# Where a seed is copied and where a shared product is added: a seven-product scheme between ScalarE and VectorE

## The chip, the cores and the metric

The kernel runs on one core of a Trainium2 chip. The core has five engines that work through queues of their own and wait for each other by semaphores: TensorE (PE, matmuls), VectorE (DVE), ScalarE (ACT), GpSimd (POOL) and SyncE (SP, which issues most DMAs). The metric is the time of one execution in microseconds; the median of three runs is compared.

## The reference

```python
def _A_ref(x, wqkv, wo):                  # x: 2048 x 640
    H = 32; Dh = D // H                   # 32 heads of 20
    W, dil = 8, 2
    qkv = ((x @ wqkv).reshape(B, S, 3, H, Dh)).transpose(2, 0, 3, 1, 4)
    q, k, v = qkv[0], qkv[1], qkv[2]
    idx = pos[:, None] - off[None, :]     # each position sees 8 keys, 2 apart, itself the last
    ...
    logits = einsum("bhsd,bhswd->bhsw", q, kg) * Dh ** -0.5
    attn = softmax(where(mask, logits, -1e9))
    o = einsum("bhsw,bhswd->bhsd", attn, vg)
    return o.transpose(0, 2, 1, 3).reshape(B, S, D) @ wo

def _B_ref(x, w1, b1, w2):                # Dense 640 -> 1728, Mish, Dense 1728 -> 640
    h = einsum("bsd,df->bsf", x, w1) + b1
    act = h * tanh(softplus(h))
    return einsum("bsf,fd->bsd", act, w2)

g = sigmoid((x * gate_w).sum(-1, keepdims=True))
return g * _A_ref(x, wqkv, wo) + (1 - g) * _B_ref(B_x, ...)
```

In this kernel both branches read the same `x`.

## The kernel before

**Matmuls.** Each float32 operand is split into a high and a low part that lie together in a `pair` buffer; a product takes three matmuls (high x high, high x low, low x high, in `mm3`, L519 to L521). ScalarE makes the high part (L451), VectorE or GpSimd the low part (L454). Matrix products are formed where possible by a seven-product scheme on 2 x 2 blocks, in which sums of blocks are multiplied and the products are added up in PSUM.

**Units.** The projection to q, k and v is worked in eight units `u`, four groups of eight heads for each half `P` of the positions, and each unit in eight slots of 128 positions. Units 2 and 3, and 6 and 7, are worked together by class `Two` (tokens `p.2.…` and `p.6.…`), in which part of the products follow the seven-product scheme, for four column blocks `j`. For each `j` there are seven steps: `a1` forms the shared product `ep` and has it copied to SBUF (`v`, an `hb` buffer), `a2` starts the sum `al`, and `be` begins with `al` plus the shared product; `a3` adds a product to `be`, `b1` and `b2` finish `al` and `be`. `c0` to `c3` do the same for the second unit from stored partial sums (`pu`, `pv`): `ga` begins with a copy (L887), `de` begins with `ga` minus the stored `v`. The value with which a PSUM bank begins is its seed here. Seeds of `Two` are made by VectorE in one instruction that reads a bank and an SBUF buffer and writes the other bank (`sum_to`, L833), 16 times in all: two for each of four `j` in both pairs of units.

When a slot's sum is done, `qkv_evac` reads it out by three ScalarE copies: k and v (320 columns, L687), q (160 columns, L689) and 16 columns of the first dense layer (`hx`, L691); a fourth (L693) only in the first unit of each half.

**Other quads.** The first dense layer is worked in quads (tokens `q.…`, classes `Quad`, `Single`, `Plain`). Their seeds already are ScalarE copies from bank to bank (`Quad.seed`, L1142), and the shared product is added by VectorE when a block is read out (`Quad.added`, L1160).

**Attention** (`attention`) runs on VectorE for each half of a unit: products with the keys (L576), sums over the 20 elements of a head (L579), maximum (L597), subtraction (L598), the exponential on ScalarE (L599), weights times the gate on ScalarE into `pw` in SBUF (L603, four instructions), sum, reciprocal and the product of both into `pg` in PSUM (L610 to L612), products with the values (L621) and their sums (L625). `qg` is a PSUM copy of two slots of q (L582); `pg` and `qg` take one bank each, and the other six are the buffers `qb` and `sb`, three each.

**Order.** `ORDER` is a list of tokens that sets the order of TensorE's work. The other engines' orders are worked out by `Plan.run`, which goes through the tasks with their ranks, estimated times and due times, and gives tasks marked "ANY" to VectorE or GpSimd (`PATIENCE` is the time after which VectorE takes one that nothing of TensorE waits for). `BANKS` names the ring (`qb` or `sb`) for some of the banks, and `NPAIR` is the number of pair buffers. After planning each engine's instructions run strictly in the planned order. Waits between engines are set by the tiles that instructions touch.

Of the kernel before, what the change touches and what calls it, by code (L numbers as in the profile page):

```python
# [17 lines left out]
KC = D // 128  # L18
# [48 lines left out]
class Plan:  # L67


    NEAR, PATIENCE = 6000, 1000  # L70
# [178 lines left out]
NPAIR, NRAW, NH = 24, 8, 6  # L249
# [4 lines left out]
BANKS = {'q1500': 's', 'p20ga': 'q', 'u04': 's', 'p21de': 's', 'u45': 's', 'p61ga': 'q', 'p63be': 'q', 'p63de': 's', 'q04ep': 's', 'q1210': 'q', 'p60de': 's', 'q1010': 'q', 'q1200': 's', 'q1111': 's', 'q02al': 's', 'u07': 's', 'u06': 's', 'q1410': 'q', 'q1501': 'q', 'u41': 's', 'q1411': 's', 'l3': 's', 'l0': 's', 'q1401': 'q', 'u46': 's', 'q1311': 's', 'q1201': 'q', 'u05': 's', 'u43': 's', 'q1001': 'q', 'u44': 's', 'q1101': 'q'}  # L254
C_RINGS = 'sqsqsqqq'
ORDER = """
u.0.6 u.0.5 last.0 u.0.4 u.0.7 q.0.0.first pieces.0.1 q.0.0.m1 q.0.1.first q.0.1.second q.0.0.second q.0.0.m3 q.0.0.m4 q.0.1.m1 wq.1 last.1 q.0.0.l2
q.0.0.m2 q.0.0.l1 pieces.0.2 q.0.1.m2 q.0.1.m4 q.0.1.m3 u.1.0 q.0.2.first u.1.2 u.1.3 u.1.1 q.0.1.l1 u.1.7 sum u.1.6 u.1.4 u.1.5 q.0.2.m1 q.0.1.l2
q.0.2.second q.0.2.m3 wa.2 q.0.2.m4 pieces.0.3 p.2.0.a1 p.2.1.a1 sum q.0.2.l2 q.0.2.m2 p.2.0.a2 p.2.0.a3 p.2.0.b1 p.2.1.a2 p.2.1.b1 p.2.1.a3 q.0.2.l1
p.2.2.a1 p.2.2.a2 p.2.2.a3 p.2.3.a1 p.2.0.b2 p.2.2.b2 p.2.3.a2 p.2.1.b2 p.2.3.b1 p.2.3.a3 q.0.3.first pieces.0.4 q.0.3.m1 q.0.3.second p.2.2.b1 wc.2  # L260
q.0.3.m3 q.0.3.m4 q.0.3.m2 p.2.3.b2 q.0.4.second q.0.3.l1 p.2.1.c0 q.0.4.first q.0.3.l2 q.0.4.m1 p.2.0.c0 q.0.4.m4 q.0.4.m3 q.0.4.m2 pieces.0.5
p.2.3.c0 x.2.0 q.0.4.l1 q.0.5.first x.2.2 q.0.5.m1 x.3.3 p.2.2.c0 x.2.1 x.3.1 q.0.4.l2 q.0.5.m4 x.3.4 x.2.3 q.0.5.m2 q.0.5.second p.2.3.c1 q.0.5.m3
p.2.3.c2 x.2.4 p.2.2.c1 q.0.5.l2 p.2.0.c1 wq.4 p.2.3.c3 x.3.2 x.3.0 q.0.5.l1 p.2.1.c1 p.2.1.c2 p.2.2.c3 p.2.2.c2 p.2.0.c3 p.2.0.c2 pieces.1.0 p.2.1.c3
third u.4.0 u.4.5 u.4.7 q.1.0.m2 sum u.4.1 wq.5 u.4.3 q.1.0.second u.4.2 sum q.1.0.m1 rest.0 u.4.6 sum rest.1 pieces.1.1 u.4.4 sum pieces.1.2 u.5.1
q.1.0.first q.1.1.first u.5.5 u.5.0 sum q.1.1.second lastw.1 q.1.1.m2 u.5.7 pieces.1.4 u.5.6 sum u.5.2 pieces.1.3 q.1.2.second q.1.1.m1 q.1.2.first
sum q.1.2.m2 u.5.4 q.1.2.m1 q.1.4.first q.1.3.first q.1.3.second pieces.1.5 last.2 u.5.3 q.1.3.m2 q.1.3.m1 q.1.4.second q.1.4.m2 forms.1.0 q.1.4.m1
last.3 wa.6 q.1.5.second p.6.1.a1 p.6.0.a1 q.1.5.m1 q.1.5.m2 p.6.0.a2 p.6.0.a3 wc.6 p.6.1.a2 p.6.0.b2 q.1.5.first p.6.2.a1 p.6.2.a2 p.6.3.a1 p.6.2.a3
p.6.0.c0 p.6.1.a3 p.6.0.b1 p.6.3.a2 p.6.0.c1 p.6.1.b1 p.6.2.b1 p.6.3.b1 p.6.2.b2 p.6.1.c0 p.6.1.c1 p.6.0.c3 p.6.3.a3 p.6.3.b2 p.6.2.c0 p.6.1.c3
p.6.3.c0 p.6.0.c2 p.6.2.c1 p.6.3.c1 p.6.2.c3 p.6.2.c2 p.6.1.c2 p.6.3.c3 p.6.1.b2 p.6.3.c2 rest.2 rest.3
# [4 lines left out]
def kernel(ctx: ExitStack, tc: tile.TileContext, x, wq, wo, w1, b1, w2, out):  # L274
# [109 lines left out]
    bound = keep.tile([1, HQ, 7], F32)  # L384
    zt = keep.tile([128, 2, 8], F32)
    gate = keep.tile([128, 2, 8], F32)
    gc = keep.tile([128, 2, 32], F32)
    gt = keep.tile([128, 2, 32], F32)
# [1569 lines left out]
```

## Time and profile before

| | |
|---|---|
| median of 3 runs | 623.35 us (620.57 to 626.04) |
| the profiled execution | 619.11 us, its span 617.3 us |
| TensorE busy | 610.7 us (99%) |
| VectorE busy | 584.2 us (95%), 551 instructions |
| ScalarE busy | 375.6 us (61%), 875 instructions |
| GpSimd busy | 335.8 us (54%) |
| DMA | 151.83 MB, 246 GB/s |

A row of a group gives the line, the engine, the operation, output and inputs by the program's names, the shape and the count, then the busy time in us and the mean ns of one, and last the idle time of the engine just before these instructions and what ended it. A row of the timeline gives start and duration in us, and in brackets the idle time ahead and what ended it. A row of the waits gives who waited for whom, us in total, times, and the longest. A row of stretches (from:to, length) gives the busy time of PE, PEld (weight loads), DVE, ACT and POOL with their counts, the granted clock of TensorE, the DMA share and GB/s.

### The profile page before, as it was taken

Reading aid. Unit: us, or ns where it says so; the run is one execution under the profiler, and the core shown is the slowest. Engines: PE = TensorE matmul, PEld = TensorE weight load, DVE = VectorE, ACT = ScalarE, POOL = GpSimd, SP = SyncE. Lnnn points to the kernel's source line nnn. Section 1 sums busy time; section 2 is a strip of 40 time slices with the busy share of each in tenths; the row PEclk is TensorE's granted clock in tenths of the full one; section 3 lists DMA queues with packets and bytes.
Section 4 is the critical chain, followed back from the end, with each engine's and each line's share of the span. In section 5 each row is a group of like instructions: output and inputs, shape, how many; then the busy total and the mean of one; then the engine's idle time right before and its main releaser. Section 6 shows DMA issues by size and latency. Waiting matters only on the chain.

```text
span 617.3 us, 9163 instructions
## 1 busy us (share of the span) xinstructions
PE 610.7 (99%) x2707; PEld 506.3 (82%) x2707; DVE 584.2 (95%) x551; ACT 375.6 (61%) x875; POOL 335.8 (54%) x309
## 2 busy tenths in 40 slices
PE   9999999999999999999999999999999999999997
PEld 7887888888878888888888888888888888888886
DVE  8799999999999999999999999999999999989955
ACT  6677747766797574654557559567686534664520
POOL 1587847868887546666887508886516824001000
PEclk9999999999999999999999999999999999999999
DMA  9773784979989679999999889868787876899613
GB/s 322 222 217 104 218 289 124 272 245 299 327 252 287 209 234 248 290 272 342 300 256 299 273 264 311 251 181 256 222 273 249 218 230 181 254 288 352 237 52 119
DMA packets 99971, 151.83 MB, mean 246 GB/s; under 512 B 11265, under 2 KB 52481, under 8 KB 99697
## 3 DMA queue, kind: packets, MB, share of 16 engines
q1 hardware_dynamic: 96560, 145.48, 73.4%
q0 software_dynamic: 3072, 5.51, 6.2%
q8 instruction: 21, 0.34, 0.2%
q10 hardware_dynamic: 288, 0.26, 0.2%
q14 instruction: 30, 0.24, 0.1%
HBM read 95.17 MB, written 55.06 MB: 243 GB/s over the span
## 4 chain that ended last, share of the span: by engine, by line
PE 91%; DVE 5%; ACT 2%; issue 1%; DMA 0%; SPq 0%; DVEq 0%; ACTq 0%
PE qb L521 16%; PE qb L520 16%; PE qb L519 16%; PE sb L519 14%; PE sb L521 13%; PE sb L520 13%; DVE pr L576 2%; DVE lg L579 1%; DVE raw L1025 1%; ACT pair L451 1%; PE qb L681 1%; PE sb L433 1%; DMA raw<-in_wq 0%; DVE pair L454 0%; PE sb L525 0%
## 5 line engine op out<-in xcount | busy, mean ns | idle before, releaser
L454 POOL TENSOR_TENSOR pair<-raw,pair 128x512 fp32r<-128x512 f32 (+3 forms) x143 | 176.1, 1254 | 99.4 <-ACT pair L451 64.1
L451 ACT ACTIVATE pair<-raw 128x512 fp32r<-128x512 f32 (+3 forms) x236 | 137.3, 606 | 56.1 <-DMA raw<-actt 12.7
L519 PE MATMUL sb<-pair 128*128 128x512 f32 (+2 forms) x386 | 149.7, 388 | 0.9 <-ACT sb L1142 0.4
L519 PE MATMUL qb<-pair 128*128 128x512 f32 (+1 forms) x387 | 150.0, 388 | 0.5 <-DVE qb L833 0.5
L521 PE MATMUL qb<-pair 128*128 128x512 f32 (+1 forms) x387 | 149.9, 387 | 0.0
L520 PE MATMUL qb<-pair 128*128 128x512 f32 (+1 forms) x387 | 149.8, 387 | 0.0
L521 PE MATMUL sb<-pair 128*128 128x512 f32 (+2 forms) x386 | 149.2, 387 | 0.0
L520 PE MATMUL sb<-pair 128*128 128x512 f32 (+2 forms) x386 | 149.2, 387 | 0.0
L621 DVE TENSOR_TENSOR pr<-kvq,pg 128x1280 f32<-128x1280 f32 x64 | 93.2, 1483 | 0.9
L576 DVE TENSOR_TENSOR pr<-kvq,qg 128x2560 f32<-128x2560 f32 x32 | 89.9, 2811 | 1.4
L625 DVE TENSOR_REDUCE kvq<-pr 128x320 f32<-128x2560 f32 x32 | 90.1, 2817 | 0.8
L579 DVE TENSOR_REDUCE lg<-pr 128x128 f32<-128x2560 f32 x32 | 90.2, 2818 | 0.8
L519 PEld LDWEIGHTS sb<-pair 128*128 128x128 f32 x386 | 72.5, 188 | 17.1 <-DVE sb L833 1.0
L519 PEld LDWEIGHTS qb<-pair 128*128 128x128 f32 x387 | 72.6, 188 | 15.4 <-DVE qb L833 0.9
L520 PEld LDWEIGHTS qb<-pair 128*128 128x128 f32 x387 | 72.7, 188 | 14.4
L521 PEld LDWEIGHTS qb<-pair 128*128 128x128 f32 x387 | 72.7, 188 | 14.3
L521 PEld LDWEIGHTS sb<-pair 128*128 128x128 f32 x386 | 72.5, 188 | 14.5
L520 PEld LDWEIGHTS sb<-pair 128*128 128x128 f32 x386 | 72.5, 188 | 14.4
L454 DVE TENSOR_TENSOR pair<-raw,pair 128x512 fp32r<-128x512 f32 (+3 forms) x93 | 65.7, 730 | 3.0 <-ACT pair L451 2.9
L1025 POOL TENSOR_TENSOR hb<-hb 128x512 f32<-128x512 f32 x34 | 44.6, 1327 | 12.2 <-DVE pg L612 3.1
L1025 POOL TENSOR_TENSOR raw<-raw 128x256 f32<-128x256 f32 (+2 forms) x35 | 34.9, 1002 | 12.2 <-DVE pg L612 3.0
L451 ACT ACTIVATE pair<-hb 128x512 fp32r<-128x512 f32 (+3 forms) x62 | 36.5, 589 | 1.7 <-PE qb L521 1.5
(167 smaller groups left out, 739.0 us busy)
## 6 DMA issues: line engine op xcount, KB each, us to landing
actt<-hb SPq DMA_DIRECT2D x52, 256.0 KB
raw<-in_w SPq DMA_DIRECT2D x47, 256.0 KB
act<-hb SPq DMA_DIRECT2D x38, 256.0 KB
raw<-in_wq SPq DMA_DIRECT2D x39, 248.0 KB
raw<-actt SPq DMA_DIRECT2D x37, 256.0 KB
raw<-act SPq DMA_DIRECT2D x29, 256.0 KB
raw<-in_x SPq DMA_DIRECT2D x27, 256.0 KB
o<-ot SPq DMA_DIRECT2D x64, 80.0 KB
```

What stands on the lines that cost most here:

```text
L433: nc.tensor.matmul(warm_banks[i % 3].t[:, :n], ones[:, :128], ones[:, :n], start=True, stop=True)
L451: a = add("ACT", act_ns(n), lambda: A.activation(hi(), raw(), AF.Copy), after, rank=rank, take=take, hold=hold)
L454: return (V if e == "DVE" else G).tensor_tensor(lo(), raw(), hi().bitcast(F32), op=OP.subtract)
L519: nc.tensor.matmul(ps, ah, bh, start=first, stop=False, skip_group_check=more)
L520: nc.tensor.matmul(ps, ah, bl, start=False, stop=False, skip_group_check=more)
L521: nc.tensor.matmul(ps, al, bh, start=False, stop=last, skip_group_check=more)
L576: return V.tensor_tensor(pr, window(kv, s0, 0), qg[:, :, None, :].to_broadcast([128, 2, W, QF]), op=OP.mult)
L579: V.tensor_reduce(lg_w[:, s0:s0 + 2], pr.rearrange("p s w (h d) -> p s w h d", d=DH), op=OP.add, axis=AX.X)
L621: V.tensor_tensor(pairs[:, s].rearrange("p k i (h d) -> p k i h d", d=DH), vw, pg[:, s0 + s].rearrange("p (k i) h -> p k i h", i=2)[:, :, ...
L625: V.tensor_reduce(q[:, s0:s0 + 2], pairs.rearrange("p s k i f -> p s f k i"), op=OP.add, axis=AX.XY)
L681: nc.tensor.matmul(ps.t[:, :n], X[0, kc].t[:, a, i * 128:(i + 1) * 128], WQ[0, kc].t[:, b, :n], start=a == b and kc == 0, stop=False)
L1025: return (V if e == "DVE" else G).tensor_tensor(t.t[:, i:i + n], a.t[:, j:j + n], b.t[:, k:k + n], op=op)
```

## The change

The seed in `Two` becomes a ScalarE copy from bank to bank (`seed`, in place of `sum_to`), in `a2` and in `c1`. The shared product is no longer part of the seed: VectorE adds or, through the stored `v`, takes it in when the slot is read out (`qkv_evac_added`), for `b2` and `c2`, 16 read-outs in all, with three additions each in place of three ScalarE copies. The sum `de` in `c3` is read out by ScalarE as before, since its seed needs `v` only through `ga`. `a2` no longer waits for `a1`.

In `attention` the weights times the gate are written into `pg` in PSUM at once, and their product with the reciprocal is made there in place; `pw` is gone. The maxima `mx` move from SBUF into the PSUM tile of `qg`. `bound`, `gc` and `gt` are smaller. With the room that this leaves there are 25 pair buffers in place of 24. `PATIENCE` goes from 1000 to 2000, and `ORDER` and `BANKS` are new lists.

```diff
-    NEAR, PATIENCE = 6000, 1000
+    NEAR, PATIENCE = 6000, 2000
...
-NPAIR, NRAW, NH = 24, 8, 6
+NPAIR, NRAW, NH = 25, 8, 6
...
-    pw = at.tile([128, 8, W, HQ], F32, name="pw")
-    pw_h = pw.rearrange("p s w h -> p s h w")
     pg = shared.tile([128, 8, W, HQ], F32, name="pg")
-    qg = shared.tile([128, 2, QF], F32, name="qg")
+    pg_h = pg.rearrange("p s w h -> p s h w")
+    qm = shared.tile([128, 512], F32, name="qg")
+    qg = qm[:, :2 * QF].rearrange("p (s f) -> p s f", f=QF)
...
-    mx = at.tile([128, 8, HQ], F32, name="mx")
+    mx = qm[:, 2 * QF:2 * QF + 8 * HQ].rearrange("p (s h) -> p s h", h=HQ)
...
-                    A.activation(pw_h[:, i], lg[:, i], AF.Copy, scale=gate[:, P, i:i + 1])
+                    A.activation(pg_h[:, i], lg[:, i], AF.Copy, scale=gate[:, P, i:i + 1])
...
-            return t, step("DVE", 430, lambda: V.tensor_tensor(pg[:, h], pw[:, h], sm[:, h, None, :].to_broadcast([128, 4, W, HQ]), op=OP.mult), [copied])
+            return t, step("DVE", 430, lambda: V.tensor_tensor(pg[:, h], pg[:, h], sm[:, h, None, :].to_broadcast([128, 4, W, HQ]), op=OP.mult), [copied])
...
+    def qkv_evac_added(u, P, hq, i, ps, done, more, held, landed):
+        kv, q, s = KV[UNIT[u]], Q[UNIT[u]], 4 * (1 - i // 4) + i % 4
...
+        def plus(to, lo, n, after):
+            return add("DVE", dve_ns(n), lambda: V.tensor_tensor(to(), ps.t[:, lo:lo + n], more()[:, lo:lo + n], op=OP.add), after,
+                       rank=SOON, kind="psum", hold=[ps, held])
+
+        def pair():
+            return V.tensor_tensor(kv[:, 7 + s], ps.t[:, QF:3 * QF].rearrange("p (a b) -> p a b", a=2),
+                                   more()[:, QF:3 * QF].rearrange("p (a b) -> p a b", a=2), op=OP.add)
+
+        a = add("DVE", dve_ns(2 * QF), pair, [done, landed] + before, rank=SOON, kind="psum", hold=[ps, held])
+        b = plus(lambda: q[:, s], 0, QF, [a])
+        c = plus(lambda: hx[:, P, i, hq], 3 * QF, RQ, [b])
...
-        def sum_to(self, to, x, y, op, n, after, yt=None):
-            yt = yt or (lambda: y.t)
-            return add("DVE", dve_ns(n) + 80, lambda: V.tensor_tensor(to.t[:, :n], x.t[:, :n], yt()[:, :n], op=op), after, rank=SOON, kind="psum",
-                       take=[to], hold=[to, x, y])
+        def seed(self, to, of, n, after):
+            return add("ACT", act_ns(n) + 60, lambda: A.activation(to.t[:, :n], of.t[:, :n], AF.Copy), after, rank=-0.5, take=[to], hold=[to, of])
...
-            self.seeded[j] = self.sum_to(be, al, self.v[j], OP.add, n, [t, self.copied[j]])
+            self.seeded[j] = self.seed(be, al, n, [t])
...
         def b2(self, j):
             t = self.products(self.be[j], j, self.xs("s4", 1, 1) + self.plain(0, 1), [self.kept[j]], self.n)
-            units[self.u].ready(4 + j, self.be[j], t)
+            v = self.v[j]
+            units[self.u].ready(4 + j, self.be[j], t, lambda: v.t, v, self.copied[j])
...
-            self.seeded[j] = self.sum_to(de, ga, v, OP.subtract, n, [t, dv], vt)
+            self.seeded[j] = self.seed(de, ga, n, [t])
+            self.last[j] = vt, v, dv
 
         def c2(self, j):
+            vt, v, dv = self.last[j]
             t = self.products(self.ga[j], j, self.plain(1, 1), [self.seeded[j]], NCOL)
-            units[self.u + 1].ready(4 + j, self.ga[j], t)
+            units[self.u + 1].ready(4 + j, self.ga[j], t, vt, v, dv)
```

Three places of the order show what this moves.

**VectorE, first steps of units 6 and 7.** L833 is the seed; `qb` and `sb` are PSUM banks, `hb` the copied shared product, `pr`, `lg`, `sm` belong to attention. Before:

```order
L576 TENSOR_TENSOR pr_276<-kvq0_269,qg_275 128x2560
L579 TENSOR_REDUCE lg_272<-pr_276 128x2x8x8
L833 TENSOR_TENSOR sb_3730<-qb_3706,hb_3701 128x496
L610 TENSOR_REDUCE sm_278<-lg_272 128x32
L833 TENSOR_TENSOR qb_3743<-qb_3726,hb_3734 128x496
L576 TENSOR_TENSOR pr_276<-kvq0_269,qg_275 128x2560
```

Now, where L707 and L703 are the three additions of a read-out:

```order
L576 TENSOR_TENSOR pr_275<-kvq0_269,qg_274 128x2560
L579 TENSOR_REDUCE lg_272<-pr_275 128x2x8x8
L707 TENSOR_TENSOR kvq1_270<-sb_3439,hb_3644 128x320
L703 TENSOR_TENSOR kvq1_270<-sb_3439,hb_3644 128x160
L703 TENSOR_TENSOR hx_81<-sb_3439,hb_3644 128x16
L610 TENSOR_REDUCE sm_276<-lg_272 128x32
```

One instruction per seed has become three per read-out, at the same kind of place, behind attention work.

**TensorE, the second steps (`c1`) of units 2 and 3.** Each row is one matmul; three rows form a product. Before, bank `sb_2046` gets a product, `sb_2049` two, and then comes `qb_2075`, whose seed is made from `sb_2046`:

```order
L521 MATMUL sb_2046<-pair_1691,pair_615 128x496
L519 MATMUL sb_2049<-pair_1639,pair_572 128x496
L520 MATMUL sb_2049<-pair_1639,pair_572 128x496
L521 MATMUL sb_2049<-pair_1639,pair_572 128x496
L519 MATMUL sb_2049<-pair_1691,pair_615 128x496
L520 MATMUL sb_2049<-pair_1691,pair_615 128x496
L521 MATMUL sb_2049<-pair_1691,pair_615 128x496
L519 MATMUL qb_2075<-pair_1661,pair_575 128x496
```

Now `qb_2120` gets its seed from `qb_2087`:

```order
L521 MATMUL qb_2087<-pair_1703,pair_613 128x496
L519 MATMUL sb_2107<-pair_1670,pair_570 128x496
L520 MATMUL sb_2107<-pair_1670,pair_570 128x496
L521 MATMUL sb_2107<-pair_1670,pair_570 128x496
L519 MATMUL sb_2107<-pair_1703,pair_613 128x496
L520 MATMUL sb_2107<-pair_1703,pair_613 128x496
L521 MATMUL sb_2107<-pair_1703,pair_613 128x496
L519 MATMUL qb_2120<-pair_1686,pair_573 128x496
```

Six matmuls stand between a product and the use of its seed, before and now; the seed between them is VectorE's before and ScalarE's now.

**VectorE, the weights of the first unit.** `pg` is the PSUM tile of the weights, `kvq0` holds the values. Before:

```order
L612 TENSOR_TENSOR pg_274<-pw_273,sm_278 128x256
L621 TENSOR_TENSOR pr_276<-kvq0_269,pg_274 128x4x2x160
L597 TENSOR_REDUCE mx_277<-lg_272 128x32
L598 TENSOR_TENSOR lg_272<-lg_272,mx_277 128x256
L621 TENSOR_TENSOR pr_276<-kvq0_269,pg_274 128x4x2x160
L625 TENSOR_REDUCE kvq0_269<-pr_276 128x320
L621 TENSOR_TENSOR pr_276<-kvq0_269,pg_274 128x4x2x160 x2
```

Now:

```order
L612 TENSOR_TENSOR pg_273<-pg_273,sm_276 128x256
L621 TENSOR_TENSOR pr_275<-kvq0_269,pg_273 128x4x2x160
L597 TENSOR_REDUCE qg_274<-lg_272 128x32
L598 TENSOR_TENSOR lg_272<-lg_272,qg_274 128x256
L621 TENSOR_TENSOR pr_275<-kvq0_269,pg_273 128x4x2x160
L625 TENSOR_REDUCE kvq0_269<-pr_275 128x320
L621 TENSOR_TENSOR pr_275<-kvq0_269,pg_273 128x4x2x160 x2
```

The rows stand alike, but between the last two L621 the other half's weights (L603 on ScalarE) now go into the same tile `pg`: in the order they wait for the first of the two, and the second waits for them.

More of the change, by code (lines that the diff above doesn't have):

```diff
@@ L261 @@
[L261 to L268, printed above, removed]
@@ L383 @@
     bias = top.tile([128, 120], F32, name="bias")
-    bound = keep.tile([1, HQ, 7], F32)
+    bound = keep.tile([1, 1, 1], F32)
     zt = keep.tile([128, 2, 8], F32)
     gate = keep.tile([128, 2, 8], F32)
-    gc = keep.tile([128, 2, 32], F32)
-    gt = keep.tile([128, 2, 32], F32)
+    gc = keep.tile([128, 32], F32)
+    gt = keep.tile([128, 32], F32)
     hx = keep.tile([128, 2, 8, NQ, RQ], F32)
```

44 lines of the change are left out of this document (30 added, 14 removed).

## The prediction

> **What bounds the kernel now.** I read the page's first part, then the waits of TensorE, its instructions in order of time around each wait, and last the groups of VectorE (DVE) and ScalarE (ACT).
>
> ```profile
> span 617.3 us, 9163 instructions
> PE 610.7 (99%) x2707; PEld 506.3 (82%) x2707; DVE 584.2 (95%) x551; ACT 375.6 (61%) x875; POOL 335.8 (54%) x309
> ...
> 250.00:300.00 50.00, 50.00 (x224) 41.83 (x223) 49.17 (x35) 27.31 (x63) 33.19 (x34) 1.00 0.98 304
> 575.00:600.00 25.00, 25.00 (x112) 20.68 (x112) 18.85 (x31) 9.39 (x16) 0.00 (x0) 1.00 0.34 123
> ```
>
> TensorE is busy from end to end at a granted clock of 1.00 (the column behind the five engines in the two rows by stretch). VectorE is nearly full too, 49.2 of 50 us in the first stretch, and has room only at the end, 18.9 of 25. A busy TensorE can still be slow, so I looked at the steps between the starts of its matmuls. They are 0.22 us for 496 columns and 0.23 for 512, and the waits are few:
>
> ```profile
> PE qb L519 <- DVE qb L833: 0.5, 1, 0.5
> PE sb L519 <- ACT sb L1142: 0.4, 1, 0.4
> PE sb L519 <- ACT sb L887: 0.4, 1, 0.4
> ...
> 60.76 0.38 PE L521 MATMUL qb<-pair,kvq 128*128 128x496 f32 x1
> 61.49 0.50 PE L519 MATMUL sb<-pair 128*128 128x512 f32 x1 [0.35 <-ACT sb L1142]
> ...
> 175.23 0.38 PE L521 MATMUL qb<-pair,kvq 128*128 128x496 f32 x1
> 175.97 0.49 PE L519 MATMUL sb<-pair 128*128 128x496 f32 x1 [0.35 <-ACT sb L887]
> ...
> 178.53 0.39 PE L521 MATMUL sb<-pair 128*128 128x496 f32 x1
> 179.45 0.49 PE L519 MATMUL qb<-pair 128*128 128x496 f32 x1 [0.53 <-DVE qb L833]
> 179.78 0.38 PE L520 MATMUL qb<-pair 128*128 128x496 f32 x1
> ...
> 183.35 0.39 PE L521 MATMUL sb<-pair 128*128 128x496 f32 x1
> 183.79 0.49 PE L519 MATMUL sb<-pair 128*128 128x496 f32 x1
> 184.12 0.38 PE L520 MATMUL sb<-pair 128*128 128x496 f32 x1
> ...
> 345.59 0.38 PE L521 MATMUL qb<-pair 128*128 128x496 f32 x1
> 346.09 0.49 PE L519 MATMUL sb<-pair 128*128 128x496 f32 x1
> 346.42 0.38 PE L520 MATMUL sb<-pair 128*128 128x496 f32 x1
> ```
>
> The first column is the start. At 178.53 the next start comes 0.92 us later instead of 0.22, and the one after it 0.33 later: a stall of 0.70 + 0.11 = 0.81 us. The same sum gives 0.33 at 183.35 and 0.39 at 345.59, and 0.6 each at 60.76 and 175.23. After the first 6 us no other step is more than 0.05 us too long. So the stalls after the start are 2.8 us together. A kernel with the same matmuls and none of these stalls would take 619.11 (this execution's own time) - 2.8 = 616.3 us. The change removes no matmul, so this is about the floor of any gain.
>
> Three of the five stalls (0.81 + 0.33 + 0.39 = 1.53 us) wait for the VectorE seed at L833. VectorE's rows show why:
>
> ```profile
> 175.99 2.81 DVE L576 TENSOR_TENSOR pr<-kvq,qg 128x2560 f32<-128x2560 f32 x1
> 178.72 0.68 DVE L833 TENSOR_TENSOR qb<-sb,pair 128x496 f32<-128x496 f32 x1
> ...
> 183.06 0.68 DVE L833 TENSOR_TENSOR sb<-sb,pair 128x496 f32<-128x496 f32 x1 [0.95 <-ACT hb L1148]
> ...
> 342.63 2.82 DVE L579 TENSOR_REDUCE lg<-pr 128x128 f32<-128x2560 f32 x1
> 345.37 0.67 DVE L833 TENSOR_TENSOR sb<-qb,hb 128x496 f32<-128x496 f32 x1
> ```
>
> Twice the seed stands behind a 2.8 us attention instruction, once behind ScalarE. The other two stalls wait for ScalarE copies, which the change leaves as they are.
>
> **The change part by part.** The seeds move to ScalarE: 16 additions of 0.67 us leave VectorE, 16 copies of about 0.59 us (the row of L1142 below, the same copy from bank to bank) come to ScalarE. At read-out 16 times three ScalarE copies (0.43 + 0.30 + 0.19) become three VectorE additions of 320, 160 and 16 columns.
>
> ```profile
> L833 DVE TENSOR_TENSOR sb<-qb,hb 128x496 f32<-128x496 f32 x7 | 4.6, 672 | 0.4 <-PE qb L521 0.4
> L833 DVE TENSOR_TENSOR sb<-sb,pair 128x496 f32<-128x496 f32 x2 | 1.4, 683 | 1.4 <-ACT hb L1148 0.9 <-ACT hx L691 0.4
> L833 DVE TENSOR_TENSOR qb<-sb,pair 128x496 f32<-128x496 f32 x2 | 1.4, 679 | 0.8 <-ACT hx L691 0.8
> L454 DVE TENSOR_TENSOR pair<-hb,pair 128x512 fp32r<-128x512 f32 x31 | 21.1, 684 | 0.0
> L454 DVE TENSOR_TENSOR pair<-hb,pair 128x128 fp32r<-128x128 f32 x1 | 0.3, 285 | 0.0
> ...
> L687 ACT ACTIVATE kvq<-qb 128x320 f32<-128x320 f32 x40 | 17.4, 434 | 31.1 <-PE qb L521 31.1
> L689 ACT ACTIVATE kvq<-qb 128x160 f32<-128x160 f32 x40 | 12.0, 301 | 0.0
> L691 ACT ACTIVATE hx<-qb 128x16 f32<-128x16 f32 x40 | 7.6, 190 | 0.0
> L687 ACT ACTIVATE kvq<-sb 128x320 f32<-128x320 f32 x24 | 10.5, 438 | 14.4 <-PE sb L521 14.3
> L1142 ACT ACTIVATE sb<-qb 128x512 f32<-128x512 f32 x5 | 2.9, 586 | 0.5 <-PE qb L521 0.4
> L603 ACT ACTIVATE pw<-lg,gate 128x64 f32<-128x64 f32 x64 | 18.2, 409 | 0.5
> ```
>
> VectorE, added: 285 ns for 128 columns and 684 for 512 make 1.04 ns a column and 0.15 us fixed, so 0.48 + 0.32 + 0.17 = 0.97 us a read-out, 15.5 us for 16. Removed: 16 x 0.67 = 10.8. Neighbours overlap by about 0.08 us (in the rows at the end of this part two of 0.64 fit into 1.28, where one alone lasts 0.68); with 48 instructions against 16, 2.5 us of the difference of 4.7 lie in such overlaps, and 2.2 stay. The idle time ahead of L833 (0.4 + 1.4 + 0.8 = 2.6 us) goes. Instructions that may run on either VectorE or GpSimd are dealt out anew: VectorE loses 4 additions of 512 columns and 2 of 496, and gets 5 splits and one addition of 256, together about -0.2. The new read-outs may wait for TensorE. I take nothing: in the order 13 of the 16 stand right behind attention work of 1.4 to 2.8 us, the same cover that made the seeds late. The other bound is the first rival.
>
> Softmax weights in place: ScalarE now writes them into the PSUM tile that VectorE reads as `pg`. In the order 11 of the 16 groups of four (L603) wait for a VectorE product (L621), and in 3 halves VectorE's next product waits for the group. In two of these a reduction of 2.8 us stands between and hides it; in the first unit two products follow each other directly, and VectorE waits for four copies of 0.41 us that now each wait for the one before: 1.6 us and some 0.3 for handing over, 1.9. The maxima share the bank of `qg`; in the order one subtraction (L598) waits for a `qg` copy on ScalarE, 0.6 us with its way. ScalarE itself has 240 us free, and groups that wait up to 1.5 us there have one unit seed close behind them. [...]
>
> VectorE's sum is 2.2 - 2.6 - 0.2 + 1.9 + 0.6 = +1.9 us. What that costs is read where VectorE is closest to TensorE's need without a seed:
>
> ```profile
> 521.95 1.28 DVE L454 TENSOR_TENSOR pair<-raw,pair 128x512 fp32r<-128x512 f32 x2
> ...
> 524.74 0.39 PE L520 MATMUL qb<-pair 128*128 128x512 f32 x1
> ```
>
> The second of the two splits, done at 523.23, is the weights' low half that TensorE reads at 524.74: 1.5 us of reserve. If 1.9 us arrive there in full, TensorE is 0.4 us later than before, and the 1.2 us gained earlier are lost too: +1.6. If the attention work, which the planner ranks behind the splits, gives way, 0. I take 0.4, nearer to 0, since VectorE has the room of the stretch from 575 us on after the attention's end.
>
> TensorE: -1.53 for the three seeds. On ScalarE the seed of one single quad has only three matmuls (0.68 us) of cover for a copy of 0.59 and two handings-over: +0.3. The unit seeds keep six matmuls or more, 1.3 us; the bound is a ScalarE queue that is late by a 1.28 us table load at the four tightest, +5. The 25th operand buffer lets loads start earlier; no TensorE wait of the trace is a DMA, so 0.
>
> Sum: -1.53 + 0.3 + 0.4 = -0.8 us, 618.3 against this execution's 619.11. The median of the runs shown, 623.35, is 4.24 above it, for reasons that no row shows; I keep that distance: **622.5 us**.
>
> **The rivals.** *Read-outs make VectorE wait (slower).* ScalarE waited 31.1 + 14.3 us for TensorE before 64 read-outs (L687), 0.71 each. If VectorE, which works in order, waits as long before its 16, that is 11.4 us, and splits and attention queue behind it. With VectorE's +1.9 and less the 1.5 of reserve this is +11.8, on top of -1.2: 634. It is slower by 1% (6.2 us) from about 0.44 us a read-out on. Against it: L833 waited 0.4 us for TensorE in 16 times.
>
> *Late VectorE is what the timed runs pay for (faster).* In the old order 11 of TensorE's waits on VectorE have under 3 us of other matmuls beyond the producer's own length, in the new one 1. If the 4.24 us above the profiled execution, and the stalls behind ScalarE copies, which themselves waited for VectorE's reading of a bank, come from that, all go: 616.3 + 0.3 = 616.6. Against it: nothing shows where those 4.24 us lie, and DMA may as well be behind them.
>
> [...]
>
> *The seeds are late on ScalarE instead (no change).* ScalarE runs table loads of 1.28 us and splits of 0.6, so three late seeds of some 0.5 us could return: 623.35.
>
> **How the numbers follow.** The forecast has 0.52, the exchange of late seeds 0.24, the faster rival 0.12, waiting read-outs 0.10, bank order 0.02. A measurement of this kernel tells about 1% from no change: 617.1 and 629.6. So faster 0.12, within 1% 0.76, slower 0.12. The range goes from 616.5, the faster rival, to 629: the highest of the runs before, 626.04, with the read-outs costing 3 us or a few late ScalarE seeds; the 634 and 661 stay outside. The forecast's own range is 619 to 626, the spread of the runs before.
>
> **What would show it.** Right: TensorE's waits name no VectorE seed, its stalls sum to 1.5 to 3 us, VectorE's busy time rises by 2 to 6 us, ScalarE's falls by 5 us or more (16 x 0.92 off, 16 x 0.59 on), and one wait of some 0.3 us follows a seed of a single quad. Wrong: the new additions have idle time "<-PE" of several us ahead of them; TensorE waits for splits (L454) between 450 and 560 us; or the stalls after 350 us are no longer zero.

## The result, and the profile after

The changed kernel takes 624.89 us (median of 22 runs, 622.29 to 626.79), the kernel before 622.50 (22 runs, 619.76 to 626.90). The ratio is 1.0035, 95% interval 1.0019 to 1.0051: slower by 0.35%, or 2.2 us. The forecast of "within 1%" holds, its sign does not: it had the change 0.8 us faster.

The profiled execution of the changed kernel took 625.64 us and lies near its median, that of before (619.11) near the lower end of its runs. The two profiles are therefore 6.5 us apart where the runs are 2.2 apart: they tell places, and the ratios tell sizes.

The page after, its first lines:

```profile
span 623.8 us, 9163 instructions
PE 611.4 (98%) x2707; PEld 505.2 (81%) x2707; DVE 586.7 (94%) x583; ACT 372.9 (60%) x841; POOL 337.4 (54%) x309
```

and the same two stretches as in the prediction (TensorE, weight loads, VectorE, ScalarE, GpSimd, clock). VectorE is as full as before in the first; in the second its work reaches further into the room at the end, 22.8 of 25 us against 18.9:

```profile
250.00:300.00 50.00, 50.00 (x224) 41.84 (x223) 49.15 (x33) 24.62 (x57) 33.69 (x35) 1.00 0.87 267
575.00:600.00 25.00, 25.00 (x112) 20.71 (x111) 22.84 (x38) 11.22 (x19) 0.82 (x1) 1.00 0.63 218
```

TensorE's waits (total us, times, longest us):

```profile
PE qb L519 <- ACT qb L910: 1.7, 1, 1.7
PE qb L519 <- ACT hx L691: 1.5, 1, 1.5
PE sb L519 <- DVE hb L1185: 1.3, 1, 1.3
PE qb L681 <- ACT pair L451: 1.1, 1, 1.1
PE qb L519 <- ACT hb L1167: 1.0, 1, 1.0
PE qb L520 <- POOL pair L454: 0.7, 1, 0.7
PE qb L519 <- ACT hb L1173: 0.2, 1, 0.2
```

The wait at L681 lies at 8.7 us, in the start, behind a load for which ScalarE waited 3.8 us in this execution, 2.0 in that of before. No seed of the units (L856) is in the list, nor a read-out on VectorE (L703, L707). In their place stand copies and read-outs on ScalarE, one addition on VectorE (L1185, `Quad.added`, which reads out a block of the first dense layer, a hidden result) and one split on GpSimd. Summed over the steps between the starts, as the prediction did, the stalls after the first 10 us are 1.27 (at 48.80), 1.73 (75.67), 0.27 (124.70), 0.31 (153.31), 1.53 (163.17), 1.98 (166.09), 0.94 (320.23), 0.50 (321.61) and 0.35 (343.66): 8.9 us against 2.8 before. After 345 us there is none. The groups of the parts that were changed (busy us, mean ns, idle us before and what ended it):

```profile
L707 DVE TENSOR_TENSOR kvq<-sb,hb 128x320 f32<-128x320 f32 x8 | 3.9, 482 | 0.9 <-PE sb L521 0.9
L707 DVE TENSOR_TENSOR kvq<-qb,pair 128x320 f32<-128x320 f32 x6 | 2.9, 482 | 0.7 <-DMA actt<-hb 0.5 <-PE qb L521 0.2
L703 DVE TENSOR_TENSOR kvq<-sb,hb 128x160 f32<-128x160 f32 x8 | 2.5, 313 | 0.0
L703 DVE TENSOR_TENSOR hx<-sb,hb 128x16 f32<-128x16 f32 x8 | 1.3, 163 | 0.0
L856 ACT ACTIVATE sb<-qb 128x496 f32<-128x496 f32 x9 | 5.1, 569 | 0.8 <-DVE hx L703 0.7
L603 ACT ACTIVATE pg<-lg,gate 128x64 f32<-128x64 f32 x64 | 20.4, 318 | 12.2 <-DVE pr L621 10.3
```

The prices were right: 0.48 + 0.31 + 0.16 = 0.96 us a read-out (estimated 0.97), 0.57 a seed (0.59). L603 is the row to look at: ScalarE waits 10.3 us for VectorE's products, where it waited for none before. Two of the new stalls, in order of time:

```profile
44.48 2.15 ACT L451 ACTIVATE pair<-raw 128x496 fp32r<-128x496 f32 x4
49.18 0.44 ACT L582 ACTIVATE qg<-kvq 128x320 f32<-128x320 f32 x1 [2.55 <-DVE pr L576]
49.55 0.58 ACT L1167 ACTIVATE hb<-qb 128x512 f32<-128x512 f32 x1
...
75.47 1.37 ACT L603 ACTIVATE pg<-lg,gate 128x64 f32<-128x64 f32 x4 [4.08 <-DVE pr L621]
76.78 0.42 ACT L687 ACTIVATE kvq<-qb 128x320 f32<-128x320 f32 x1
77.09 0.29 ACT L689 ACTIVATE kvq<-qb 128x160 f32<-128x160 f32 x1
77.28 0.18 ACT L691 ACTIVATE hx<-qb 128x16 f32<-128x16 f32 x1
```

At 49 us the copy L1167, for which TensorE waits, stands behind a `qg` copy that waits 2.55 us for VectorE. At 75 us a read-out (L687 to L691), whose bank TensorE needs, stands behind weights that wait 4.08 us for VectorE. The first theory was therefore that the weights in place cost the time. It fell, and most of those after it.

### The profile page after: what moved, and what is told of

Its sections match the earlier page's. It is cut to its first block, busy times and chain, and to the rows that moved or that the text cites. A ratio compares the mean times of both kernels' runs of the same rounds, so it can differ in the third digit from the quotient of the medians.

```text
span 623.8 us, 9163 instructions
## 1 busy us (share of the span) xinstructions
PE 611.4 (98%) x2707; PEld 505.2 (81%) x2707; DVE 586.7 (94%) x583; ACT 372.9 (60%) x841; POOL 337.4 (54%) x309
## 4 chain that ended last, share of the span: by engine, by line
PE 47%; DMA 5%; ACT 2%; issue 1%; SPq 0%; POOL 0%; DVE 0%; DVEq 0%; ACTq 0%
PE sb L521 8%; PE sb L520 8%; PE sb L519 8%; PE qb L519 8%; PE qb L520 8%; PE qb L521 8%; DMA actt<-hb 1%; DMA raw<-in_wq 1%; DMA raw<-in_w 1%; DMA act<-hb 1%; ACT hb L1173 1%; ACT pair L451 0%; SPq L484 0%; PE sb L525 0%; PE qb L526 0%
## 5 line engine op out<-in xcount | busy, mean ns | idle before, releaser
L454 POOL TENSOR_TENSOR pair<-raw,pair 128x512 fp32r<-128x512 f32 (+4 forms) x136 | 169.0, 1257 | 83.5 <-ACT pair L451 46.9
L519 PE MATMUL sb<-pair 128*128 128x512 f32 (+1 forms) x406 | 157.1, 387 | 0.1
L520 PE MATMUL sb<-pair 128*128 128x512 f32 (+1 forms) x406 | 157.0, 387 | 0.0
L521 PE MATMUL sb<-pair 128*128 128x512 f32 (+1 forms) x406 | 157.0, 387 | 0.0
L519 PE MATMUL qb<-pair 128*128 128x512 f32 (+1 forms) x367 | 142.3, 388 | 2.0 <-ACT qb L910 1.7
L520 PE MATMUL qb<-pair 128*128 128x512 f32 (+1 forms) x367 | 142.1, 387 | 0.7 <-POOL pair L454 0.7
L521 PE MATMUL qb<-pair 128*128 128x512 f32 (+1 forms) x367 | 142.0, 387 | 0.0
L621 DVE TENSOR_TENSOR pr<-kvq,pg 128x1280 f32<-128x1280 f32 x64 | 93.5, 1483 | 2.4 <-ACT pg L603 1.5
L519 PEld LDWEIGHTS sb<-pair 128*128 128x128 f32 x406 | 76.2, 188 | 15.9 <-ACT sb L1167 0.5
L520 PEld LDWEIGHTS sb<-pair 128*128 128x128 f32 x406 | 76.2, 188 | 15.2
L521 PEld LDWEIGHTS sb<-pair 128*128 128x128 f32 x406 | 76.2, 188 | 15.2
L519 PEld LDWEIGHTS qb<-pair 128*128 128x128 f32 x367 | 68.9, 188 | 16.8 <-ACT qb L910 2.1
L520 PEld LDWEIGHTS qb<-pair 128*128 128x128 f32 x367 | 68.9, 188 | 14.5 <-POOL pair L454 1.1
L521 PEld LDWEIGHTS qb<-pair 128*128 128x128 f32 x367 | 68.9, 188 | 13.4
L454 DVE TENSOR_TENSOR pair<-raw,pair 128x512 fp32r<-128x512 f32 (+3 forms) x100 | 68.4, 706 | 4.3 <-ACT pair L451 4.2
L1050 POOL TENSOR_TENSOR hb<-hb 128x512 f32<-128x512 f32 x38 | 50.6, 1335 | 36.9 <-ACT hb L1173 9.9
L1050 POOL TENSOR_TENSOR raw<-raw 128x256 f32<-128x256 f32 (+2 forms) x37 | 38.7, 1058 | 14.4 <-DMA raw<-in_w 3.6
L454 POOL TENSOR_TENSOR pair<-hb,pair 128x512 fp32r<-128x512 f32 (+2 forms) x26 | 31.6, 1222 | 13.9 <-ACT pair L451 8.2
```

The source lines that it names most:

```text
L454: return (V if e == "DVE" else G).tensor_tensor(lo(), raw(), hi().bitcast(F32), op=OP.subtract)
L519: nc.tensor.matmul(ps, ah, bh, start=first, stop=False, skip_group_check=more)
L520: nc.tensor.matmul(ps, ah, bl, start=False, stop=False, skip_group_check=more)
L521: nc.tensor.matmul(ps, al, bh, start=False, stop=last, skip_group_check=more)
L621: V.tensor_tensor(pairs[:, s].rearrange("p k i (h d) -> p k i h d", d=DH), vw, pg[:, s0 + s].rearrange("p (k i) h -> p k i h", i=2)[:, :, ...
L1050: return (V if e == "DVE" else G).tensor_tensor(t.t[:, i:i + n], a.t[:, j:j + n], b.t[:, k:k + n], op=op)
```

## The experiments: each part alone, in the old order

Two kinds of kernels were made: such as keep the order of every engine instruction for instruction and change one thing in it, and such as let the planner make a new order. All ratios are to the kernel before. The letters are those of the theories in the expectations.

**Weights and maxima in place, nothing else.**

```diff
-    pw = at.tile([128, 8, W, HQ], F32, name="pw")
...
-    qg = shared.tile([128, 2, QF], F32, name="qg")
+    qm = shared.tile([128, 512], F32, name="qg")      # qg and mx in one bank
...
-                    A.activation(pw_h[:, i], lg[:, i], ...
+                    A.activation(pg_h[:, i], lg[:, i], ...
```

> The kernel before with one part of the change: the gate-weighted softmax numerators are written into the PSUM tile pg and the maxima into the bank of qg; the order of every engine, the banks and the buffers stay as before. Theory A (weights in place tie ScalarE to VectorE's products, and TensorE's banks are read out late behind them): ScalarE's L603 waits for VectorE's L621, 8 us or more in all, TensorE gets new stalls behind ScalarE read-outs, and the time is 1.5 to 3 us above before. Theory B (the new order and bank table give ScalarE's copies less cover): 0 +- 0.7 us against before, although L603 waits. Theory C (VectorE's three read-out additions): 0 +- 0.7 us.

0.9988 (0.9967 to 1.0008). ScalarE does wait, and VectorE for ScalarE too:

```profile
ACT pg L603 <- DVE pr L621: 12.4, 8, 3.7
DVE pr L621 <- ACT pg L603: 3.0, 2, 1.5
```

But TensorE's list of waits stays that of before, and the time is not told from it. Theory A, which asked for 1.5 to 3 us more, is wrong for this order: 12.4 us of waiting on ScalarE cost nothing that shows, and none of the instructions behind them is one that TensorE waits for.

**The engines exchanged, nothing else.** The seeds are ScalarE copies and the read-outs VectorE copies at the same places of the old order; the shared product is left out, so nothing is held longer.

```diff
-  V.tensor_tensor(to.t[:, :n], x.t[:, :n], yt()[:, :n], op=op)
+  A.activation(to.t[:, :n], x.t[:, :n], AF.Copy)
-  A.activation(kv[:, 7 + s], ps.t[:, QF:3 * QF]..., AF.Copy)        (also q, hx)
+  V.tensor_scalar(kv[:, 7 + s], ps.t[:, QF:3 * QF]..., 1.0, None, op0=OP.mult)
```

> The kernel before with its order, banks and buffers kept instruction for instruction, only the engines exchanged in place: the 16 seeds are ScalarE copies, the 16 read-outs are VectorE copies out of the bank. The shared product is left out of the sums, so nothing is held longer. Theory D (the exchange of engines is worth what was predicted, and the loss comes from holding the shared product until the read-out, which deals buffers and order anew): 0 to 1.5 us under before, no TensorE wait for a VectorE seed. Theory E (the exchange itself costs): 2 us or more above before, with new TensorE stalls behind seeds or read-outs. Theory F (any change of the planner's inputs costs several us under an order that was found for others): as D, since the order is kept.

1.0003 (0.9976 to 1.0031): +0.2 us where 0 to -1.5 was expected, with an interval from -1.5 to +1.9 us that leaves theory D standing. TensorE's waits for the seeds are on ScalarE now, 0.85 us and 0.76 (before, 0.53 and less, for VectorE), and at 327 us there is a stall of 1.5 us that the kernel before does not have, 1.07 of them a wait for a GpSimd split. **Both together**, again in the old order:

> The kernel before in its own order with both parts of the change at once: ScalarE seeds and VectorE read-outs (copies, the shared product left out of the sums, so that nothing is held longer) and weights and maxima in PSUM. All of the change but its order, bank table, patience and 25th buffer. If the order carries the loss (theories F, G and H): -1.5 to +1 us against before. If the two parts cost only together: 1.5 us or more above before.

1.0032 (1.0012 to 1.0052): all of the change but its order, bank table, patience, 25th buffer and the longer holding of the shared product is as slow as the changed kernel. So a loss of this size comes without the new order, and theories F, G and H, which laid it there, miss this run: they asked for +1 us at most, 2.0 were measured (0.7 to 3.2). The run is not told from the exchange alone: the two intervals overlap. ScalarE's and TensorE's rows of it at the place where the seeds were late before:

```profile
177.01 2.18 ACT L451 ACTIVATE pair<-raw 128x512 fp32r<-128x512 f32 x4
179.09 0.56 ACT L839 ACTIVATE qb<-sb 128x496 f32<-128x496 f32 x1
...
181.31 1.28 ACT L1154 ACT_TABLE_LOAD   x1
182.60 0.72 ACT L1154 ACTIVATE hb<-hb,bias 128x512 f32<-128x512 f32 x1
183.23 0.67 ACT L1154 ACTIVATE hb<-sb,bias 128x512 f32<-128x512 f32 x1
183.80 0.42 ACT L689 ACTIVATE kvq<-qb 128x320 f32<-128x320 f32 x1
184.12 0.58 ACT L839 ACTIVATE sb<-sb 128x496 f32<-128x496 f32 x1
...
179.71 0.49 PE L519 MATMUL qb<-pair 128*128 128x496 f32 x1 [0.85 <-ACT qb L839]
184.75 0.49 PE L519 MATMUL sb<-pair 128*128 128x496 f32 x1 [0.76 <-ACT sb L839]
...
326.71 0.49 PE L519 MATMUL qb<-pair 128*128 128x496 f32 x1 [0.93 <-ACT pair L451]
328.26 0.49 PE L520 MATMUL qb<-pair 128*128 128x496 f32 x1 [1.06 <-POOL pair L454]
```

L839 is the seed on ScalarE. It stands behind four splits (2.18 us), and behind a table load and two hidden results. TensorE waits 0.85 and 0.76 us for it, where it waited 0.53 and less for VectorE. This is the prediction's rival of seeds that are late on ScalarE, row by row. The exchange alone has the same two waits, so they are not what sets the two runs apart. The stall at 326 us is 2.5 us in its steps here, 1.5 in the exchange alone, and behind it TensorE's steps are 0.41 to 0.43 us from 328.87 to 331.81 us, where they were 0.23 up to 325.40 (last section).

**VectorE's added work taken away again.** The same kernel, each read-out cut to 16 columns:

```diff
-  V.tensor_scalar(to, src, 1.0, None, op0=OP.mult)
+  V.tensor_scalar(to[some], src[some], 1.0, None, op0=OP.mult)       # 16 columns
```

> The run with both parts in the old order, each VectorE read-out cut to 16 columns (the rest of the result is left out), which takes some 7 us of work from VectorE. Theory I: no stall at 325 us; what stays are the seeds that are late on ScalarE (2 us against 1.1 before); 0 to 1.5 us above before, 1 to 3 under the run with whole read-outs. If VectorE's load isn't it: the stall at 325 us stays, within 0.7 us of that run.

0.9968 (0.9946 to 0.9989): 4.0 us under the run with whole read-outs, and the intervals do not meet. VectorE's busy time goes from 585.7 to 578.4 us. The stall at 326 us is gone, and one of the late seeds is shorter:

```profile
PE sb L519 <- ACT sb L842: 0.8, 1, 0.8
PE qb L519 <- ACT qb L842: 0.4, 1, 0.4
PE sb L519 <- ACT sb L1151: 0.4, 1, 0.4
```

So in the old order the time hangs on the work that the read-outs bring to VectorE, in the direction of theory C: 7.3 us of it less are worth 4.0 us. That takes away more than the change added: VectorE ends 5.8 us under the kernel before (584.2), and the time 2 us under it. Whether 7.3 us less of VectorE's other work would have won as much was not tried, and the cut also gives each bank free earlier, by an estimate from the two busy times 0.46 us (7.3 us over 16 read-outs).

**VectorE late by itself.** To see whether lateness alone does this, one attention reduction was done twice in the kernel before:

```diff
+                if red_count[0] == 13:
+                    V.tensor_reduce(lg_w[:, s0:s0 + 2], pr..., op=OP.add, axis=AX.X)
                 V.tensor_reduce(lg_w[:, s0:s0 + 2], pr..., op=OP.add, axis=AX.X)
```

> The kernel before with one attention reduction (L579, 2.8 us, the one at 204 us) done twice on VectorE; nothing else is changed. Theory I (VectorE's added work reaches TensorE at 325 us: GpSimd's operations wait for VectorE, hidden results and ScalarE's splits stand behind them): TensorE waits at 325 us for the split L454, the new stall is 1.5 to 4 us, and the time 1.5 to 4 us above before. The prediction's reading (the reserve is the 1.5 us at 524 us, and attention work gives way): no stall at 325 us, 0 to 1.3 us above before.

0.9992 (0.9970 to 1.0015), and no stall at 326 us. Theory I falls in this form: one lump of 2.8 us at 204 us is free within 0.9 us, as the prediction's reading said. What the 16 read-outs do and a lump does not stays open. They stand at the places where a bank is to be handed on: in the run with both parts, two seeds on ScalarE waited 2.7 and 2.4 us for a VectorE read-out of their bank. But the exchange alone, whose loss is not shown, has one such wait of 2.7 us, the run with short read-outs one of 2.2, and TensorE has no stall behind any of them. Nor is the stall at 326 us a sure mark: it is in the profile of the exchange alone, and in that of the last run below, where VectorE's work is untouched. Single stalls also come and go with the execution: this run's profile has one of 0.9 us at 108 us, ahead of the doubled reduction, where the kernel before has none.

## The experiments: the order

**The exchange undone inside the new order.** The mirror of the exchange above: seeds as VectorE copies, read-outs as ScalarE copies, the shared product left out.

```diff
-  add("ACT", ..., lambda: A.activation(to.t[:, :n], of.t[:, :n], AF.Copy), ...)
+  add("ACT", ..., lambda: V.tensor_scalar(to.t[:, :n], of.t[:, :n], 1.0, None, op0=OP.mult), ...)
```

> The changed kernel with its order, banks and buffers kept, only the engines exchanged back in place: the 16 seeds are VectorE copies, the 16 read-outs ScalarE copies, the shared product left out of the sums. Theories D and F: 0 to 3 us above the changed kernel, with TensorE waiting for VectorE seeds again, since their order has them behind attention work. Theory E: 2 us or more under the changed kernel.

1.0117 (1.0080 to 1.0154): 5.1 us above the changed kernel (0.0082 x 622.5). Its waits:

```profile
PE qb L519 <- ACT qb L912: 3.3, 1, 3.3
PE sb L519 <- DVE sb L858: 2.0, 2, 1.6
PE qb L519 <- ACT hx L691: 1.5, 1, 1.5
PE qb L520 <- POOL pair L454: 1.2, 1, 1.2
```

The seeds are late on VectorE again (L858), which makes 2.6 us of stalls by their steps. In the new order the exchange is worth 5 us, in the old one nothing that shows. The other three rows are the changed kernel's stalls at 166, 75 and 320 us: they are there whoever makes the seeds. Not all of the 5 us lie at seeds: the wait at 166 us is 3.3 us in place of 1.7, with read-outs back on ScalarE.

**One buffer less, and the weights apart again.** `NPAIR` 24 instead of 25, and the same with `pw` and `mx` in SBUF, as the freed room allows (both runs have one order).

> The changed kernel with 24 operand buffers instead of 25. All three theories: within 0.7 us of the changed kernel, 2 to 3 us above before; if the 25th buffer matters, loads are later here and it is slower still.

> The changed kernel with 24 operand buffers and with weights and maxima in SBUF again, the order of every engine the same as in the run with 24 buffers. Theory A: 1.5 to 3 us below that run, at before's time or under it; L603 waits for no VectorE product. Theories B and C: within 0.7 us of that run.

1.0137 (1.0115 to 1.0159) and 1.0152 (1.0118 to 1.0186). Weights in place or apart: no difference that shows, as in the old order. The buffer less costs 6 us. No wait of TensorE there is for a load: it waits for VectorE (`hb` 2.5 us, a split 2.1) and for ScalarE, in another order that the planner makes with 24 buffers. What fewer buffers cost by themselves can't be told from that order.

**The old order with other buffers.** ScalarE seeds and VectorE additions with the shared product under the order table of before (24 operand and 7 hidden-result buffers, weights in SBUF); the kernel before with weights in place and a seventh hidden-result buffer; and this with the shared product held until the read-out.

```diff
-NPAIR, NRAW, NH = 24, 8, 6
+NPAIR, NRAW, NH = 24, 8, 7
-   return pe_add(..., take=take, hold=[ps] + bs)                    (third kernel only)
+   return pe_add(..., take=take, hold=[ps] + bs + list(kept))
```

> The kernel with ScalarE seeds and VectorE read-outs, with the order, bank table and patience of before; weights in SBUF as before; the maxima share the bank of qg; 24 operand buffers and 7 hidden-result buffers instead of 6, since the shared product is now held until its read-out. Theory A: 0.5 to 1.5 us below before, since the VectorE seeds no longer stall TensorE. Theory B: the same as A, or a little above, since this order was not made for it. Theory C: 1.5 to 3 us above before, with TensorE waiting for VectorE's splits or the attention's end.

> The kernel before with weights in place (worth -1.2 us, not told from 0) and 7 hidden-result buffers instead of 6: the control of the next run. Theories D and E: within 1.5 us of before. Theory F: 4 us or more above before, although it has a buffer more.

> The run before this one, with the VectorE seeds and ScalarE read-outs of before, but the buffer of the shared product is given back only when the matmuls ahead of the read-out are done, as the change must. Theory D: 5 to 20 us above the control, with ScalarE waiting for loads or for hidden results longer, and TensorE for ScalarE. Theory E: as the control. Theory F: as the control within 3 us, in either direction.

1.0328 (1.0303 to 1.0354), 1.0471 (1.0420 to 1.0522) and 1.0395 (1.0343 to 1.0446). A seventh buffer, with the weights in place that cost nothing alone, makes the kernel before 29 us slower, and the shared product held on top of that makes it 5 us faster, not slower as theory D (holding costs) asked. Theory F holds in all five kernels that the planner ordered anew under a table found for other inputs: each is 8 to 29 us slower, whatever the input was that changed. This fits the change coming with a table of its own, and it means that such kernels tell little about their edit, about holding too.

**Single places of the new order.** First the weights of the first two units in a part of `hx` that is free until unit 4; then the third `qg` copy moved behind L1167; then both; then also the product at 161 us moved behind the two additions L1185, and a GpSimd combination behind the split at 319 us.

```diff
-  A.activation(pg_h[:, i], lg[:, i], ...)
+  A.activation((spare_h if u < 2 else pg_h)[:, i], lg[:, i], ...)
...
ACT:  - L582 qg   L1167 hb<-qb         + L1167 hb<-qb   L582 qg
DVE:  - L576 pr   L1185 hb x2          + L1185 hb x2    L576 pr
POOL: - L1050 hb  L454 pair            + L454 pair      L1050 hb
```

> The changed kernel with its order kept; only in the first two units the weights go to a part of hx that is not used until unit 4, instead of into pg. Theory G (the new order puts ScalarE behind VectorE at a few places with bank read-outs right behind, and each such place costs its stall): L603 at 75 us no longer waits 4 us for L621, TensorE's stall of 1.7 us there is gone, and the time is 1 to 2 us under the changed kernel, 0.5 to 1.5 us above before. Theory H (a stall taken away returns at the next late load, split or VectorE result): within 0.5 us of the changed kernel, 2 to 3 us above before, with later stalls longer.

> The changed kernel with one ScalarE instruction exchanged with its neighbour: the third qg copy (at 49 us, it waited 2.55 us for VectorE) goes behind the read-out L1167 that TensorE waits for. Theory G: the stall of 1.2 us at 49 us is gone and the time 0.7 to 1.5 us under the changed kernel, 1 to 2 us above before. Theory H: within 0.5 us of the changed kernel.

> Both edits of the two runs before this one together. Theory G: 2 to 3.5 us under the changed kernel, that is within 1 us of before. Theory H: within 0.7 us of the changed kernel, 2 to 3 us above before.

> The run with both edits, and two more exchanges of neighbours in the changed order: on VectorE the attention product of 2.8 us at 161 us goes behind the two additions L1185, of which TensorE waited for the first 1.3 us; on GpSimd the combination at 318.5 us goes behind the split L454, for which TensorE waited 0.7 us. Theory G (the time above before is the sum of such late places): these two stalls are gone as well, and the time is at before's or up to 2 us under it. Theory H (a stall taken away returns at a later one): 1 to 2.5 us above before, as the changed kernel, with other waits in the list.

In this order: 1.0039 (1.0016 to 1.0063), 1.0033 (1.0000 to 1.0067), 1.0020 (0.9994 to 1.0047), 1.0042 (1.0019 to 1.0064). Each wait that an edit aims at is gone from the profile, and none of the four kernels is told from the changed one. The stall at 75 us grew from 1.7 to 2.4 us when the one at 49 us was taken away; with four places mended, TensorE waits 3.1 us at 163 us instead of 1.3 and 1.7 close by, and 0.6 us for a seed at 379 us where nothing was before. Theory H, that stalls return at a later place, fits. Theory G, that they add up, asked for the time of before or less with four places mended, which lies outside that run's interval; the first three runs alone would not decide it.

**Which engine, in the new order.** The read-outs cut to 16 columns as above; and every Exp and Mish replaced by a copy, which takes 25 table loads of 1.28 us from ScalarE, with the same in the kernel before as control.

```diff
-  V.tensor_tensor(to(), ps.t[:, lo:lo + n], more()[:, lo:lo + n], op=OP.add)
+  V.tensor_tensor(to()[:, :16], ps.t[:, lo:lo + 16], more()[:, lo:lo + 16], op=OP.add)
...
-  A.activation(hb.t, src.t, AF.Mish, bias=bias[:, fc:fc + 1])
+  A.activation(hb.t, src.t, AF.Copy)
```

> The changed kernel, each VectorE read-out cut to 16 columns of the three pieces (the rest left out), order kept. Theory I: 1.5 to 3 us under the changed kernel, within 1 us of before, with the waits at 163 us and 320 us shorter. If the loss lies in the changed order's own late places (75 us, 163 us, 166 us), whatever VectorE does later: within 1 us of the changed kernel.

> The changed kernel with every Exp and Mish replaced by a plain copy (the functions are left out), order kept: 25 table loads of 1.28 us, 32 us of ScalarE's time, are gone. Theory J (in the changed order ScalarE is what TensorE ends up waiting for): 3 to 6 us under the changed kernel, 1 to 3 under before, and the gain is at least 2 us larger than that of the next run. Theory H (VectorE, loads, stores and ScalarE all stand close, so a stall taken from one returns at another): 0 to 2 us under the changed kernel, and no more than the next run gains.

> The control: the kernel before with every Exp and Mish replaced by a plain copy, order kept. Both theories: 0 to 2 us under before, since its stalls behind ScalarE copies sum to 1.2 us.

1.0024 (1.0004 to 1.0045), 0.9997 (0.9971 to 1.0022) and 0.9983 (0.9959 to 1.0008). In the new order VectorE's read-outs are not shown to cost: 4.4 us less on VectorE (586.7 to 582.3) bring 0.7 us, not told from none, nor from 2. 37 us less on ScalarE (372.9 to 336.0) bring 2.4 us there and 1.1 in the old order; the stalls from 318 us on are gone, those at 49, 75, 163 and 166 us stay. Theory J asked for 2 us more than the control; 1.3 were measured, which the intervals tell neither from 0 nor from 2.

## Why the prediction was wrong, and where it was right

- **The three late seeds, -1.53 us.** Right in the new order: no L856 is among the waits, and undoing the exchange brings 2.6 us of seed stalls back. In the old order two of the three stay late, on ScalarE, as the rival of late ScalarE seeds said, and grow (1.1 and 1.0 us by the steps with both parts, for 0.81 and 0.33); the third, at 345 us, goes.
- **The single quad's seed, +0.3.** Right: 0.31 us at 153.31.
- **The read-outs waiting for TensorE.** The first rival's 0.71 us each did not come: 1.1 us in all before the 16 (rows of L707; the two that are not shown waited for nothing), 0.07 each, far under the 0.44 from which it decides.
- **Busy times.** VectorE +2.5 us (2 to 6 predicted). ScalarE -2.7 instead of -5 or more: the 64 weight copies take 20.4 us in all against 18.2, which the prediction left out. Each is shorter (318 ns against 409), but they overlap less: four last 1.37 us where they lasted 1.14.
- **Weights in place.** VectorE's waits for L603 are there (1.5 us once, 3.0 in the old order; 1.9 predicted). The chance of 0.02 for bank order and the 661 us that stay outside the range would need each of the 16 halves to wait 1.9 + 0.6 us on VectorE; no run shows that: VectorE waited for L603 once in the changed kernel (1.5 us), twice in the old order (3.0 us together), and L598 for a `qg` copy once in the changed kernel, 0.8 us. The sentence that ScalarE's groups "wait up to 1.5 us" was wrong: up to 4.1. In the old order and in the order with 24 buffers the part costs no time that shows, so its price is not seen to be part of the error.
- **VectorE's +1.9 us for 0.4: the term that failed in the old order.** The cost was read at 524 us, where a split had 1.5 us of reserve, and there it was nearly right: in the kernels of the old order with the parts of the change, TensorE loses at most 0.15 us in its steps at that place and has no wait there. But the time hangs on the read-outs earlier on: 7.3 us of them are worth 4.0, while a lump of 2.8 us elsewhere is free. So a reserve read at one place did not price work at another. For the changed kernel itself the term is not shown wrong, since shorter read-outs bring 0.7 us there, not told from none.
- **"The other two stalls wait for ScalarE copies, which the change leaves as they are": the step that failed in the changed kernel.** It looked at the 16 seeds and read-outs in the new order and took the rest of that order as costing what the old one did, a term of 0. The prediction's sign of being right was stalls of 1.5 to 3 us; 8.9 were seen, and 7.95 of them stand at 49, 75, 163, 166 and 320 to 322 us, at none of the 16 seeds or read-outs. All of these are in the profile of the new order with short read-outs as well. Those at 49 and 75 us could have been looked for: a `qg` or weight copy on ScalarE that waits for VectorE, with a copy or read-out of a bank behind it. In the runs the kernel is 2.2 us slower, not the 6.5 that the two profiles are apart.
- **The 25th buffer, 0.** By itself not measured; with 24 the planner makes an order that costs 6 us more.
- **The distance of 4.24 us** between profile and median, carried over as a constant, was none: the changed kernel's profiled execution lies 0.75 us above its median.

What is shown: both parts together cost 2 us in the old order, where the weights in place alone cost nothing and the exchange alone lies anywhere from 1.5 us faster to 1.9 slower, and shorter read-outs on VectorE take that loss away. In the new order the seeds are no longer late and other stalls stand in their place. What makes these cost 2 us stays open: no single place, and neither VectorE's read-outs nor ScalarE's table loads, was shown to carry it. No kernel that computes all of the reference was measurably faster than before; the nearest is before with the weights in place, 0.9988.

## What to carry to other kernels

Where a program's order is planned, exchange engines inside the unchanged order first: it tells the edit's worth from that of the new plan, which here was 8 to 29 us where the edit was 2. Read an engine's reserve at every kind of consumer, not only where it is smallest for one: a bank that is handed on to another engine may be a deadline too (two seeds on ScalarE waited 2.7 and 2.4 us for one). And where stalls return at other places, as here, a stall taken away is not time won until a run says so.

## What was not expected of the hardware

In one run a wait of 2.14 us was followed by slower steps of TensorE, 1.3 us more in seven of them. It is the run with the moved `qg` copy (start, duration; the steps between starts are what to read):

```profile
73.86 0.39 PE L529 MATMUL sb<-kvq,pair 128*128 128x512 f32 x1
76.39 0.49 PE L527 MATMUL qb<-pair,kvq 128*128 128x496 f32 x1 [2.14 <-ACT hx L699]
...
77.39 0.59 PE L528 MATMUL qb<-pair,kvq 128*128 128x496 f32 x1
77.77 0.61 PE L529 MATMUL qb<-pair,kvq 128*128 128x496 f32 x1
78.18 0.61 PE L527 MATMUL qb<-pair,kvq 128*128 128x496 f32 x1
78.60 0.61 PE L528 MATMUL qb<-pair,kvq 128*128 128x496 f32 x1
...
80.25 0.61 PE L529 MATMUL qb<-pair,kvq 128*128 128x496 f32 x1
```

One microsecond after the wait, the step becomes 0.38 to 0.42 us instead of 0.22, and is so up to 80.25 at least: seven steps in 2.86 us, which at 0.22 take 1.54. The wait of 1.70 us in the changed kernel was not followed by it: the steps from 168.52 to 173.98 us are 0.22 to 0.24 us there, and the granted clock from 168 to 176 us is 1.00. In the run with both parts in the old order the granted clock falls from 1.00 (300 to 326 us) to 0.76 in the 7 us after 326 us:

```profile
326.00:333.00 7.00, 5.23 (x15) 4.00 (x16) 6.90 (x4) 5.96 (x13) 7.00 (x7) 0.76 0.72 213
```

There two waits stand close together, 0.93 us ahead of 326.71 and 1.06 us ahead of 328.26. What makes TensorE slower after some waits and not after others was not shown. The spread between executions goes with the granted clock: of the 132 executions of the kernel before that the ratios of the experiments rest on, the 92 with a mean granted clock of 0.998 or more have a median of 621.8 us, the other 40 one of 624.6. With both parts in the old order 8 of 12 executions were below 0.998, of the kernel before beside them 6 of 22.
